# Moving the third head group's PV beside the fourth's in a fused attention and GEGLU kernel

## The chip, the cores and the metric

The kernel runs on one core of a Trainium2 chip. The metric is device time in microseconds (us) for one execution; lower is better. A core has a matrix engine (TensorE, PE in the profile, with its weight loads as PEld), a vector engine (VectorE, DVE), a scalar engine (ScalarE, ACT), a general engine (GpSimd, POOL) and a queue engine that issues DMAs (SyncE, SP). The engines run side by side, each through its own list of instructions in order, and wait for each other on semaphores. Matmuls write to PSUM, which has eight banks; a bank holds 128 x 512 float32. Only ACT and DVE copy results out of it here.

## The reference: a layernorm, a windowed attention and a GEGLU network, summed

```python
xn = layernorm(x)                                   # x: 1 x 2048 x 448, bf16
q, k, v = split_heads(xn @ wqkv)                    # 16 heads of 28
scores = einsum("bhqd,bhkd->bhqk", q, k) * 28**-0.5
mask = (i - j >= 0) & (i - j < 256)                 # sliding window of 256 keys
o = einsum("bhqk,bhkd->bhqd", softmax(where(mask, scores, -1e9)), v) @ wo
f = (gelu(xn @ w_gate) * (xn @ w_up)) @ w_down      # 448 -> 1792 -> 448
out = x + o + f
```

Each query sees at most 256 keys. The kernel takes the exponential without subtracting a maximum, and sums of the exponentials come from a column of ones that stands beside v.

## The kernel before

**Blocks.** The 2048 rows are worked in four blocks of 512 (`qb`, the loop at L740). Each block has an attention part (`attention`, L531) and a gate part (`gated`, L422). The down projection of a block (`gen_down`, L345) adds the attention output and the feed-forward output of that block in one PSUM bank, and is done in the attention part of the next block, as filling; that of the last block stands at the end of the kernel.

**Attention of a block.** The 16 heads are four groups of four. Scores, exponentials and masks are made in steps (`steps_of`, L473): nine in block 0, ten in the others. A step is a set of score matmuls into one buffer `sc` of four PSUM banks (L600), one exponential on ACT over 128 x 2048 (L604, tile `p_sb`, a ring of five buffers), then masks: in block 0 on POOL (L528), in the others three multiplications on DVE (L518), which are issued at the start of the following step. There is one `sc` buffer in this part (`score_pool(1)`), so the scores of a step wait for the exponential of the step before. In between TensorE works through `plan`, a list written out by hand with one entry per step: so many matmuls or pairs of matmuls of a generator. `(d, 5)` is five matmuls of the down projection of the block before (L359, tile `po`), `(u, 7)` or `(w, 7)` seven pairs of projections for the next block (L319, L333) or of early up pairs (`gen_up`, L401, tile `ue`). An entry `"sums"`, `"inverse"` or `"scale"` issues a part of the softmax division: `sums` (L539) transposes `oc` and takes the reciprocal on DVE, `inverse` (L547) transposes back on DVE, `scale_o` (L536) multiplies on POOL (L537) into `oN`.

**PV.** `pv(g)` (L562) multiplies the exponentials of a group with v (L570, tile `ov`). In block 0 it takes one PSUM bank and DVE copies it to `oc` (L580). In the other blocks it takes two, one for each half of the array, and `add_halves` (L553) copies the first on ACT (L554) and adds the second on DVE (L555). For group 2 and 3 of those blocks (`g > 1`) this pair is put in the list `behind` and issued at the next `flush`. `oc` has one buffer for even groups (tag `wa`) and one for odd groups (tag `wb`). The dictionary `pvs` (L585) says ahead of the scores of which step a group's PV stands: groups 0, 1 and 2 at steps 4, 6 and 9 (in block 0 at 4, 6 and 8). Group 3's PV is issued in `rest` (L629), which `gated` calls between the first gate matmuls and the first gelu (L439).

**PSUM banks.** Four banks belong to `sc`; after the last step the same four become two buffers `gt` of two banks each for the gate matmuls (`score_pool(2)`). The other four (`spare`) are handed out in turn by `take` and returned by `give` (L203, L214): to projections, down tiles, PVs and up pairs. Both lists are worked through when the program is built; on the chip a taker waits for the engine that last read the bank.

**Gate part.** A pair `p` is two of the 14 chunks of 128 hidden features. `gate(p)` is seven pairs of matmuls into `gt` (one chunk in each half of the array) and a gelu on ACT (L441); `up(p)` is seven pairs into two banks `u`; `end(p)` multiplies the two on DVE (L446 or L449) and calls `hook`, which issues parts of the softmax division by way of `after` (L639) and DMA transposes. Pairs in `early` have their up part done in attention already: 0 to 4 in block 0, 1 to 6 in block 3, none in blocks 1 and 2. The order of the gate part is written out at L454 to L471.

**Tile shapes.** A matmul can use a part of the array. The down projection and the last q projection use all of it (128 rows x 128 columns), projections, gate and up pairs half of it each (64 x 128), scores 32 x 64 (32 x 128 in block 0) and PVs 64 x 32 (128 x 32 in block 0).

Of the kernel before, what the change touches and what calls it, by code (L numbers as in the profile page):

```python
# [26 lines left out]
def kernel(  # L27
# [11 lines left out]
    nc = tc.nc  # L39
# [382 lines left out]
    def gated(qb, early, last_v, flush, hook):  # L422

        hT = hTs[qb]
        us, ges = {}, {}

        def up(p):
            if p in early:
                return
            us[p] = [take("u") for _ in range(2)]  # L430
            for c in range(7):
                chunk(us[p], wu, p, qb, c)

        def gate(p):
            gt = phase[0].pool.tile([P, 2, QB], f32, name="gt", tag="s")
            for c in range(7):
                chunk([gt[:, i, :] for i in range(2)], wg, p, qb, c)
            if not p:
                last_v()  # L439
            ges[p] = work.tile([P, 4, QB], bf16, name="p_sb", bufs=5)[:, 0:2, :]  # L440
            nc.scalar.activation(out=ges[p][:, :, :], in_=gt[:, :, :], func=ACT.Gelu_apprx_tanh)  # L441

        def end(p):
            ge = ges.pop(p)
            if p in early:
                nc.vector.tensor_tensor(out=both(hT, p), in0=ge[:, :, :], in1=both(hT, p), op=ALU.mult)  # L446
            else:
                for i, u in enumerate(us.pop(p)):
                    nc.vector.tensor_tensor(out=hT[:, p + 7 * i, :], in0=ge[:, i, :], in1=u, op=ALU.mult)  # L449
                    give(u)  # L450
                    flush()
            hook(2 * p)

        up(0)  # L454
        gate(0)
        end(0)
        gate(1)
        if 1 in early:
            end(1)
            gate(2)  # L460
            up(2)
        else:
            gate(2)
            up(1)
            end(1)
            up(2)
        end(2)
        for p in range(3, 7):
            gate(p)
            up(p)  # L470
            end(p)  # L471
# [59 lines left out]
    def attention(qb, plan):  # L531
        oN = blk.tile([P, 4, QB], bf16, name="oN")
        oNs[qb] = oN
        parts, copied, inverses, later, fresh, behind = {}, [], [], [], [], []

        def scale_o(g, oc, inv):  # L536
            nc.gpsimd.tensor_tensor(out=oN[:, g, :], in0=oc[:, :], in1=inv, op=ALU.mult)  # L537

        def sums():  # L539

            g, oc = copied.pop(0)
            l1 = work.tile([P, 16, 32], f32, name="l1", tag="wc", bufs=2)
            nc.vector.transpose(out=l1[:, :, :].rearrange("p a b -> p (a b)"), in_=oc[:, :])
            nc.vector.reciprocal(out=inv_all[:, 4 * qb + g, :], in_=l1[:, :, Dh])
            inverses.append((g, oc, l1))

        def inverse():  # L547

            g, oc, l1 = inverses.pop(0)
            nc.vector.transpose(out=l1[:, :, :], in_=inv_all[:, 4 * qb + g, :].unsqueeze(2).to_broadcast([P, 16, 32]))  # L550
            later.append((g, oc, l1[:, :, :].rearrange("p a b -> p (a b)")))

        def add_halves(oc, ov):  # L553
            nc.scalar.copy(out=oc[:, :], in_=ov[0][:, :])  # L554
            nc.vector.tensor_tensor(out=oc[:, :], in0=oc[:, :], in1=ov[1][:, :], op=ALU.add)  # L555
            give(*ov)

        def flush():
            while behind:
                add_halves(*behind.pop(0))  # L560

        def pv(g):  # L562

            ov = [take("ov") for _ in range(2 if qb else 1)]
            todo = parts.pop(g)
            for n, (half, kt, q0, nq, col, p_sb) in enumerate(todo):
                k0 = 64 * half if half else 0
                r = slice(k0, k0 + (P if half is None else 64))
                for j in range(4):
                    nc.tensor.matmul(ov[half or 0][32 * j:32 * j + 32, q0:q0 + nq], lhsT=v_sb[r, kt, 4 * g + j, :],  # L570
                                     rhs=p_sb[r, j, col:col + nq], start=n == (half or 0), stop=n + len(ov) >= len(todo),
                                     tile_position=(k0, 32 * j), skip_group_check=True)
            oc = work.tile([P, QB], f32, name="oc", tag="wb" if g % 2 else "wa", bufs=1)
            if qb:
                if g > 1:
                    behind.append((oc, ov))
                else:
                    add_halves(oc, ov)
            else:
                nc.vector.tensor_copy(out=oc[:, :], in_=ov[0][:, :])  # L580
                give(*ov)
            copied.append((g, oc))

        steps = list(steps_of(qb))
        pvs = {4: 0, 6: 1, 9: 2} if qb else {4: 0, 6: 1, 8: 2}  # L585
        for i, (scores, ncol, edges) in enumerate(steps):
            assert (qb, scores[-1][0]) in done
            if i in pvs:
                pv(pvs[i])
            while fresh:  # L590
                apply_masks(*fresh.pop(0))
            if qb == 3 and i - 1 in pvs:
                sums()
            ss = phase[0].pool.tile([P, 4, QB], f32, name="sc", tag="s")
            p_sb = work.tile([P, 4, QB], bf16, name="p_sb", bufs=5)
            for g, half, kt, q0, nq, col in scores:
                k0, nk = (64 * half, 64) if half is not None else (0, P)
                for j in range(4):
                    r = slice(32 * j, 32 * j + Dh)
                    nc.tensor.matmul(ss[k0:k0 + nk, j, col:col + nq], lhsT=kT[r, g, kt * P + k0:kt * P + k0 + nk],  # L600
                                     rhs=qT[r, g, ring(qb).start + q0:ring(qb).start + q0 + nq], start=True, stop=True,
                                     tile_position=(32 * j, k0), skip_group_check=True)
                parts.setdefault(g, []).append((half, kt, q0, nq, col, p_sb))
            nc.scalar.activation(out=p_sb[:, :, 0:ncol], in_=ss[:, :, 0:ncol], func=ACT.Exp, scale=SCALE)  # L604
            flush()
            if qb:
                fresh.append((p_sb, edges))
            else:
                for m in edges:
                    masked(p_sb, *m)  # L610
            while later:
                scale_o(*later.pop(0))
            for n in plan[i]:
                if n == "sums":
                    sums()
                elif n == "inverse":
                    inverse()
                elif n == "scale":
                    scale_o(*later.pop(0))
                if not isinstance(n, tuple):  # L620
                    if callable(n):
                        n()
                    continue
                for _ in range(n[1]):
                    next(n[0], None)
            if qb == 3 and i - 2 in pvs:
                inverse()

        def rest():  # L629
            while fresh:  # L630
                apply_masks(*fresh.pop(0))
            if not qb:
                scale_o(*later.pop(0))
                sums()
                inverse()
                scale_o(*later.pop(0))
            pv(3)

        def after(f):  # L639
            if inverses:  # L640
                inverse()
                scale_o(*later.pop(0))
            elif copied:
                sums()

        return rest, after, flush


# [25 lines left out]
    pvs = [take("pv", D)]  # L674
# [65 lines left out]
    for qb in range(NB):  # L740
# [4 lines left out]
        if qb == 0:  # L745
# [4 lines left out]
            plan = [[(u, 2), ahead, (u, 1)], [lambda: v_dense(2, pvs[2]), (u, 2), ahead2, (u, 1)],  # L750
                    [lambda: spare.append(spare.pop(1)), (u, 2), ahead3, (u, 4)], [lambda: stat(8), (u, 11)],
                    [lambda: stat(9), (u, 7), lambda: stat(10), (u, 7), lambda: fill_pads(True)], ["sums", (u, 7)],
                    ["inverse", "scale", (w, 11)], [(w, 7)],
                    [(w, 10), lambda: stat(11), lambda: rstd(8, 4), "sums", "inverse", (w, 7)]]
        else:
            d = gen_down(qb - 1)
            if qb < 3:
                u = gen_pairs(qb + 1, (("v", 0), ("k", 0), ("v", 2), ("k", 1), ("k", 2)))
                plan = [[(d, 14)], [(d, 11)], [(d, 11)], [(u, 7)], [(d, 18)], ["sums", (u, 7), "inverse"], [(u, 12)],
                        [(u, 9)], [lambda: q_last(qb + 1, nc.vector.tensor_copy), (d, 5), "sums", "inverse"], [(d, 13)]]  # L760
                if qb == 1:
                    for i in range(4):
                        plan[i].insert(0, lambda t=12 + i: stat(t))
# [4 lines left out]
            else:  # L768
                new_hT(3)
                early = (1, 2, 3, 4, 5, 6)  # L770
                u = gen_up(3, early)
                plan = [[(d, 14)], [(d, 4), (u, 5)], [(u, 9)], [(u, 7)], [(d, 18)], [(u, 7)], [(d, 13)], [(d, 5), (u, 7)],
                        [(u, 7)], [(d, 18)]]
        if qb in (1, 2):
            swap(qb + 1)
        score_pool(1)
# [171 lines left out]
```

## Time and profile before

| what | value |
|---|---|
| median of 3 runs | 216.26 us (216.24 to 216.41) |
| the profiled execution | 216.39 us |
| its span, first to last instruction | 214.7 us |
| TensorE busy | 209.1 us (97%) |
| DVE busy | 160.8 us (75%) |
| ACT busy | 130.6 us (61%) |
| POOL busy | 46.8 us (22%) |

The profile is of one execution; its rows give the start from the begin of the span, the length, the engine, the line of the kernel, and the tiles as output <- input. The difference between the execution's time and its span, 1.69 us, lies before the first and behind the last instruction. The chain of work that ended last is followed back from the last instruction, at each step to what released it or to the instruction before it on its engine. Matmuls overlap, and their ends are modelled, so the distance between starts tells more than the length of one.

### The profile page before, as it was taken

The numbers are of one execution on the slowest core, as the hardware profiler recorded it, in microseconds if no ns is written. First come the engines' busy times: TensorE is split into PE (matmuls) and PEld (weight loads), VectorE is DVE, ScalarE is ACT, GpSimd is POOL, SyncE is SP. The second block draws the span as 40 slices with busy tenths as digits, with TensorE's granted clock in tenths as the row PEclk, the third lists the DMA queues.
The fourth block names the chain that finished last, engine by engine and source line by source line (L and its number), as shares of the span: only waits on it lengthen the run. The fifth ranks groups of instructions, "written<-read, shape, count | busy, mean of one in ns | idle before, by whom it ended". The sixth has DMA issues, their size and how long they took to land.

```text
span 214.7 us, 6354 instructions
## 1 busy us (share of the span) xinstructions
PE 209.1 (97%) x2722; PEld 101.6 (47%) x2722; DVE 160.8 (75%) x357; ACT 130.6 (61%) x121; POOL 46.8 (22%) x78
## 2 busy tenths in 40 slices
PE   7999999999999999999999999999999999999993
PEld 2433444444454444444445436544444444444892
DVE  7899986999866995698546899576449699587621
ACT  4699587666767976513767897432678576466000
POOL 5287658331000211022000202022000021114001
PEclk9999999999999999999999999999999999999999
DMA  6999579993411101003230000200000000000011
GB/s 185 263 232 219 106 176 249 224 308 63 98 50 23 43 3 32 17 11 62 51 95 24 24 3 0 62 5 3 0 26 0 24 3 24 21 3 2 24 34 39
DMA packets 23297, 15.21 MB, mean 71 GB/s; under 512 B 8960, under 2 KB 23136, under 8 KB 23264
## 3 DMA queue, kind: packets, MB, share of 16 engines
q1 hardware_dynamic: 22320, 14.47, 30.0%
q8 instruction: 22, 0.36, 0.7%
q10 hardware_dynamic: 944, 0.29, 0.5%
q14 instruction: 11, 0.09, 0.2%
HBM read 9.03 MB, written 2.18 MB: 52 GB/s over the span
## 4 chain that ended last, share of the span: by engine, by line
PE 94%; DVE 1%; ACT 1%; DMA 1%; issue 1%; DVEq 0%; ACTq 0%
PE po L359 26%; PE gt L401 20%; PE u L401 12%; PE ue L401 8%; PE sc L600 6%; PE pq L333 5%; PE ov L570 5%; PE pv L319 4%; PE pq L190 2%; PE pk L333 1%; PE pv L190 1%; DMA x_sb<-in_A_x_dram 1%; ACT p_sb L604 1%; DVE st L154 1%; PE s L190 1%
## 5 line engine op out<-in xcount | busy, mean ns | idle before, releaser
L604 ACT ACTIVATE p_sb<-sc 128x2048 bf16<-128x2048 f32 x39 | 73.3, 1880 | 22.5 <-PE sc L600 15.7
L537 POOL TENSOR_TENSOR oN<-oc,l 128x512 bf16<-128x512 f32 x16 | 22.6, 1410 | 137.5 <-DVE l L550 137.5
L441 ACT ACTIVATE p_sb<-gt 128x1024 bf16<-128x1024 f32 x28 | 28.7, 1025 | 36.5 <-PE gt L401 29.6
L359 PE MATMUL po<-wd,hT 128*128 128x448 bf16 (+1 forms) x266 | 47.9, 324 | 0.0
L401 PE MATMUL gt<-xnT,wg 64*128 64x512 bf16 x224 | 45.3, 376 | 0.0
L401 PE MATMUL gt<-xsw,wg 64*128 64x512 bf16 x168 | 40.4, 376 | 0.0
L449 DVE TENSOR_TENSOR hT<-p_sb,u 128x512 bf16<-128x512 bf16 x34 | 22.0, 682 | 18.0 <-PE u L401 10.3
L518 DVE TENSOR_TENSOR p_sb<-p_sb,masks 128x256 bf16<-128x256 bf16 (+1 forms) x90 | 30.2, 391 | 4.5 <-ACT p_sb L604 4.5
L359 PEld LDWEIGHTS <-hT 128*128 128x128 bf16 x266 | 24.6, 98 | 16.2 <-issue 1.2
L401 PEld LDWEIGHTS <-wg 64*128 64x128 bf16 x392 | 19.5, 94 | 22.0 <-issue 0.2
L401 PEld LDWEIGHTS <-wu 64*128 64x128 bf16 x392 | 18.6, 94 | 23.1 <-issue 3.3
L401 PE MATMUL u<-xnT,wu 64*128 64x512 bf16 x136 | 28.2, 376 | 0.0
L401 PE MATMUL u<-xsw,wu 64*128 64x512 bf16 x102 | 24.6, 376 | 0.0
L367 DVE TENSOR_TENSOR res<-po,x_sb 128x448 bf16<-128x448 f32 (+1 forms) x17 | 10.1, 593 | 18.0 <-PE po L359 17.9
L401 PE MATMUL ue<-xnT,wu 64*128 64x512 bf16 x88 | 18.3, 377 | 0.0
L600 PE MATMUL sc<-qT,kT 28*64 28x320 bf16 (+7 forms) x648 | 16.4, 261 | 0.1
L401 PE MATMUL ue<-xsw,wu 64*128 64x512 bf16 x66 | 16.4, 377 | 0.0
L528 POOL TENSOR_SCALAR_AFFINE_SELECT p_sb<-p_sb 128x512 bf16<-128x512 bf16 (+1 forms) x21 | 14.2, 700 | 6.5 <-ACT p_sb L604 6.4
L359 PE MATMUL po<-wo,oN 128*128 128x448 bf16 (+1 forms) x76 | 15.1, 323 | 0.0
L600 PEld LDWEIGHTS <-kT 28*64 28x64 bf16 (+1 forms) x648 | 7.5, 102 | 12.6 <-issue 10.9
L418 DVE CAST hT<-ue 128x512 bf16<-128x512 f32 x20 | 12.7, 677 | 0.5 <-PE ue L401 0.4
L570 PE MATMUL ov<-p_sb,v_sb 64*32 64x320 bf16 (+7 forms) x648 | 11.7, 256 | 0.0
(102 smaller groups left out, 267.4 us busy)
## 6 DMA issues: line engine op xcount, KB each, us to landing
out_dram<-res SPq DMA_DIRECT2D x15, 112.0 KB
x_sb<-in_A_x_dram SPq DMA_DIRECT2D x3, 448.0 KB
wd<-in_B_w_down_dram SPq DMA_DIRECT2D x3, 448.0 KB
xsw<-xnT SPq DMA_DIRECT2D x6, 192.0 KB
wu<-in_B_w_up_dram SPq DMA_DIRECT2D x2, 560.0 KB
wg<-in_B_w_gate_dram SPq DMA_DIRECT2D x2, 448.0 KB
wg<-in_B_w_gate_dram SPq DMA_DIRECT2D x2, 336.0 KB
wraw<-in_A_wqkv_dram SPq DMA_DIRECT2D x2, 252.0 KB
```

What stands on the lines that cost most here:

```text
L333: nc.tensor.matmul(ps, lhsT=w.rearrange("p h d -> p (h d)"), rhs=xchunk(qb, hi, c, qb * QB, QB), start=c == 0, stop=c == 6, tile_position= ...
L359: nc.tensor.matmul(po[:, a:b], lhsT=x[:, k, cs], rhs=wt[:, k, lo + a:lo + b], start=(n == a == 0), stop=(n == len(terms) - 1), skip_group_ ...
L401: nc.tensor.matmul(ps, lhsT=w[64 * hi:64 * hi + 64, c, p * P:(p + 1) * P], rhs=xchunk(qb, hi, c, qb * QB, QB), start=c == 0, stop=c == 6, ...
L418: copy(out=hTs[qb][:, p + 7 * i, :], in_=us[i])
L441: nc.scalar.activation(out=ges[p][:, :, :], in_=gt[:, :, :], func=ACT.Gelu_apprx_tanh)
L449: nc.vector.tensor_tensor(out=hT[:, p + 7 * i, :], in0=ge[:, i, :], in1=u, op=ALU.mult)
L518: nc.vector.tensor_tensor(out=reg, in0=reg, in1=m, op=ALU.mult)
L528: nc.gpsimd.affine_select(out=reg, in_=reg, pattern=mid + [[1 if diag else -1, min(w, P)]], compare_op=ALU.is_ge, fill=0.0, base=0 if diag ...
L537: nc.gpsimd.tensor_tensor(out=oN[:, g, :], in0=oc[:, :], in1=inv, op=ALU.mult)
L570: nc.tensor.matmul(ov[half or 0][32 * j:32 * j + 32, q0:q0 + nq], lhsT=v_sb[r, kt, 4 * g + j, :], rhs=p_sb[r, j, col:col + nq], start=n == ...
L600: nc.tensor.matmul(ss[k0:k0 + nk, j, col:col + nq], lhsT=kT[r, g, kt * P + k0:kt * P + k0 + nk], rhs=qT[r, g, ring(qb).start + q0:ring(qb) ...
L604: nc.scalar.activation(out=p_sb[:, :, 0:ncol], in_=ss[:, :, 0:ncol], func=ACT.Exp, scale=SCALE)
```

## The change

Four edits that belong together.

- `pvs` loses group 2, and `rest` issues `pv(2)` directly ahead of `pv(3)`: both now stand behind the matmuls of gate pair 0. Only group 3 (`g > 2`) is put in `behind`; the copy and the add of group 2 follow its PV at once.
- In `gated` gate pairs 0 and 1 stand first, then up pair 0, then the rest as before.
- `rest` no longer makes the sums, the inverse and the scaling of group 2 in block 0; the ends of the gate pairs do, as in the other blocks.
- Block 0: three pairs of matmuls move from step 8 to step 7. Blocks 1 and 2: one down matmul moves from step 9 to step 8. Block 3: three up pairs move from step 7 to step 8.

```diff
@@ gated
+        gate(0)
+        gate(1)
         up(0)
-        gate(0)
         end(0)
-        gate(1)
         if 1 in early:
             end(1)
             gate(2)
-            up(2)
         else:
             gate(2)
             up(1)
             end(1)
-            up(2)
+        up(2)
         end(2)
@@ pv
             if qb:
-                if g > 1:
+                if g > 2:
                     behind.append((oc, ov))
@@ attention
-        pvs = {4: 0, 6: 1, 9: 2} if qb else {4: 0, 6: 1, 8: 2}
+        pvs = {4: 0, 6: 1}
@@ rest
             while fresh:
                 apply_masks(*fresh.pop(0))
-            if not qb:
+            while later:
                 scale_o(*later.pop(0))
-                sums()
-                inverse()
-                scale_o(*later.pop(0))
+            pv(2)
             pv(3)
@@ plan, block 0 (steps 7 and 8)
-                    ["inverse", "scale", (w, 11)], [(w, 7)],
-                    [(w, 10), lambda: stat(11), lambda: rstd(8, 4), "sums", "inverse", (w, 7)]]
+                    ["inverse", "scale", (w, 11)], [(w, 10)],
+                    [lambda: stat(11), (w, 7), lambda: rstd(8, 4), "sums", "inverse", (w, 7)]]
@@ plan, blocks 1 and 2 (steps 8 and 9)
-                        [(u, 9)], [lambda: q_last(qb + 1, nc.vector.tensor_copy), (d, 5), "sums", "inverse"], [(d, 13)]]
+                        [(u, 9)], [lambda: q_last(qb + 1, nc.vector.tensor_copy), (d, 6), "sums", "inverse"], [(d, 12)]]
@@ plan, block 3 (steps 7 and 8)
-                plan = [[(d, 14)], [(d, 4), (u, 5)], [(u, 9)], [(u, 7)], [(d, 18)], [(u, 7)], [(d, 13)], [(d, 5), (u, 7)],
-                        [(u, 7)], [(d, 18)]]
+                plan = [[(d, 14)], [(d, 4), (u, 5)], [(u, 9)], [(u, 7)], [(d, 18)], [(u, 7)], [(d, 13)], [(d, 5), (u, 4)],
+                        [(u, 10)], [(d, 18)]]
```

## The prediction, made before the changed kernel was built

> **What bounds the kernel now.** The first view is the page: part 1 (busy time), the clock row of part 2 and the shares of the chain in part 4.
>
> ```profile
> span 214.7 us, 6354 instructions
> ...
> PE 209.1 (97%) x2722; PEld 101.6 (47%) x2722; DVE 160.8 (75%) x357; ACT 130.6 (61%) x121; POOL 46.8 (22%) x78
> ...
> PEclk9999999999999999999999999999999999999999
> ...
> PE 94%; DVE 1%; ACT 1%; DMA 1%; issue 1%; DVEq 0%; ACTq 0%
> ```
>
> TensorE is busy for 209.1 of 214.7 us, its clock is full in every slice, and the chain of work that ended last runs on it for 94% of the span. So there are nearly no holes to close: a change can win only if TensorE spends less time on the same matmuls. The diff adds and removes no matmul, so I looked in the chain for time that TensorE spends without streaming columns. The second view is that chain, in order of time, at the end of attention of block 1, where the diff cuts (start, length, line):
>
> ```profile
> 76.14 0.38 PE sc L600 x16
> ...
> 77.48 0.95 PE po L359 x5
> 78.43 0.68 PE ov L570 x40
> 79.11 0.34 PE sc L600 x16
> 79.46 2.58 PE po L359 x13
> 82.04 1.63 PE u L401 x14
> 83.66 1.51 PE gt L401 x14
> 85.17 0.66 PE ov L570 x40
> 85.83 3.14 PE gt L401 x28
> ```
>
> The reader is to see three things. There is no gap: from 77.48 on each piece begins where the last ends. Seven pairs of gate or up matmuls take 1.51 us when they follow others of the same tile shape (the gt at 83.66), so a pair of 512 columns streams in 1.51/7 = 0.216 us. But the same seven pairs take 1.63 at 82.04, where they follow the down projection, which uses the whole array: **a change of tile shape costs 1.63 - 1.51 = 0.12 us**. The PV pieces say the same: by the code a PV of blocks 1 to 3 streams 512 + 512 + 256 = 1280 columns in each half of the array, which at 0.216 per 512 is 0.54 us, and the piece lasts 0.68 (behind po) or 0.66 (behind gt). So 0.14 us of a PV is its change of shape, in whichever row it is booked.
>
> **The change, part by part.** *The third group's PV goes behind the fourth's gate.* Before, step 9 runs po, ov, sc, po and later gt, ov, gt: six changes of shape, counting po to u. After, it is po, sc, po, gt, ov, ov, gt: five. What goes is one change per block: 0.68 - 0.54 = 0.14 us in each of blocks 1 to 3. No row of before shows two PVs side by side, so I bound that seam. At best it costs nothing, as u to gt does, and a change might cost as much as the dearest first up pair, 1.68 (below) - 1.51 = 0.17. At worst the seam costs a full change and the block gains nothing. I take a seam of zero, that is 0.14, because gt behind u is the nearest row: another tile, another PSUM bank, the same shape. The Trainium skill, TensorEngine Tiling (Array Packing), under Key Properties, says that changing the tiling mode, "not just tile", drains TensorE; that would make the seam free. No row here shows that seam itself.
>
> *Block 0.* Here there is a second loss. The timeline shows it on TensorE and then on DVE (start, length, engine, line, count, in brackets the idle time before and who ended it); behind them stand further rows of the chain, which this and the next parts use.
>
> ```profile
> 35.01 0.38 PE L333 MATMUL pq<-xnT,wqp 64*128 64x512 bf16 x1
> 35.34 0.37 PE L333 MATMUL pk<-xsw,wsq 64*128 64x512 bf16 x1
> ...
> 38.16 0.38 PE L401 MATMUL gt<-xnT,wg 64*128 64x512 bf16 x1
> 38.36 0.40 PE L401 MATMUL gt<-xsw,wg 64*128 64x512 bf16 x2
> ```
>
> ```profile
> 32.66 1.16 DVE L226 CAST v_sb<-pv 128x448 bf16<-128x448 f32 x2 [0.60 <-PE pv L319]
> 34.59 0.69 DVE L580 COPY oc<-ov 128x512 f32<-128x512 f32 x1 [0.78 <-POOL oN L537]
> ```
>
> ```profile
> 31.62 0.33 PE sc L600 x8
> ...
> 33.49 0.60 PE ov L570 x16
> 34.09 0.33 PE sc L600 x8
> ...
> 40.03 0.60 PE ov L570 x20
> ...
> 132.48 1.68 PE u L401 x14
> ...
> 174.67 0.35 PE sc L600 x16
> ...
> 177.69 0.35 PE sc L600 x16
> 178.04 1.62 PE ue L401 x14
> 179.66 0.68 PE ov L570 x40
> 180.34 0.34 PE sc L600 x16
> 180.69 3.53 PE po L359 x18
> ```
>
> The two halves of a pair normally start together. At 35.01 pq starts, but its partner pk only at 35.34, and at 38.16 and 38.36 they are still apart; only the PV, a change of shape, brings them together. Following `take` and `give` by hand, pk of group 1 gets the bank in which the third group's PV has just been. That bank is free when L580 has copied it, 34.59 + 0.69 = 35.28, and L580 was held for 0.78 by POOL's scaling of L537, which releases the `wa` buffer. In the chain, from the end of the scores (34.09 + 0.33 = 34.42) to the PV stand 3 + 7 + 7 pairs of projections and 7 of gates: 24 x 0.216 = 5.18, so 39.60, and with 0.12 for the change of shape 39.72. The PV started at 40.03: **0.31 us lost**. After the change no PV stands there. Group 1 takes two banks of the second v pair, copied out by 32.66 + 1.16 = 33.82, and the skew has no cause. The PV of block 0 streams 384 + 384 + 256 + 128 = 1152 columns, 0.48 us, of a piece of 0.60, so its change of shape is 0.12. Block 0 gains 0.12 + 0.31 = 0.43.
>
> *Fills moved.* A PV stood between two score steps as cover for the exponential that must end before the next scores can use the single score buffer. Where it goes, the interval shrinks, and the fills of the diff put part of it back. How short may it be? ACT's rows in block 3, where the intervals are shortest (start, length):
>
> ```profile
> 160.58 1.88 ACT L604 ACTIVATE p_sb<-sc 128x2048 bf16<-128x2048 f32 x1 [0.54 <-PE sc L600]
> 163.00 1.88 ACT L604 ACTIVATE p_sb<-sc 128x2048 bf16<-128x2048 f32 x1 [0.54 <-PE sc L600]
> ```
>
> 163.00 - 160.58 = 2.42: 1.88 of exponential and 0.54 until the next starts. I take that for the floor; it may be a little lower, which would only help. Blocks 1 and 2, step 8: scores stand at 76.14 and 79.11, 2.97 apart; without the PV (0.68) and with one more po (2.58/13 = 0.20) it is 2.49, above the floor by 0.07. Blocks 0 and 3, from the chain's rows above: block 0, step 7: 34.09 - 31.62 = 2.47, less 0.60 and with three pairs (0.65) 2.52: above. Block 3, step 7: 177.69 - 174.67 = 3.02, less three pairs 2.37: **below by 0.05**, a stall of that size. Step 8: 180.34 - 177.69 = 2.65, less 0.68 and with 0.65, 2.62: above. So the fills cost 0.05 in all, at most 0.2 if my intervals are 0.1 too long in blocks 1 and 2.
>
> *First gate instead of the first up pair behind the last step.* Gate 0 uses the score buffer's banks, so it waits for the last exponential, where up pair 0 did not. In block 1 the last scores move from 79.11 to 79.11 - 0.48 = 78.63; gate 0 follows after 0.34 of scores and 12 po at 2.58/13, that is 2.72, at 81.35. The exponential begins at most 0.54 behind the start of the scores (the floor leaves 0.54 for release and scores together) and ends by 78.63 + 0.54 + 1.88 = 81.05. Cover of 0.30: no cost; without it, each us of delay costs a us in blocks 1 and 2. What the edit moves on ACT is one copy of the PV (L554), which now stands ahead of the first gelu instead of ahead of the table load; gate 2 is the first to need that gelu, some 4 us later (two PVs, gate 1, up 0). Up pair 0 takes the banks of the third group's PV, and between that PV and it lie the other PV (0.54) and gate 1 (1.51), 2.05 in all, against a copy on ACT and an add on DVE, by L580's 0.69 some 1.4 (an estimate from that row). No DMA is moved past another; the stores and the k3 round trip keep their order.
>
> *Sums, inverse and scaling in block 0* move from ahead of the fourth PV to the ends of gate pairs, as in the other blocks. They leave DVE's queue where PV copies wait; TensorE needs the scaled result only in block 1's first down projection. Cost nothing.
>
> *Sum:* 0.43 + 0.14 + 0.14 + (0.14 - 0.05) = 0.80 us. The profiled execution took 216.39 us (the span and 1.69 around it), so 215.59 in its terms. The median of the runs is 216.26, 0.13 lower; I take the 0.80 from that: **215.5 us**, 0.37% faster. By the ends for the seam: all at zero gain in blocks 1 to 3 and in block 0, 0.31 - 0.05 = 0.26, so 216.0; all at 0.17, 0.94, so 215.3. Less than 0.2%, 0.43 us, can hardly be told from no change here, so faster means under 215.83.
>
> **The rivals.** *A: a PV is bound by its instructions, not by columns and a drain.* Then two side by side last twice one, and only the bank wait of block 0 goes: 216.26 - 0.26 = 216.0, no change by the bound. For it: the weight loads of one PV alone, in block 2, last 0.56.
>
> ```profile
> 128.80 0.56 PEld L570 LDWEIGHTS <-v_sb 64*32 64x32 bf16 x48 [0.37 <-issue]
> ```
>
> Against it: block 0's PV with less than half of the matmuls (16 in the row at 33.49, 40 at 179.66) takes 0.60 to 0.68, and scores of 8 matmuls 0.33 to the 0.35 of 16: the length follows columns, not instructions. The Trainium skill, TensorE: Matmul & The Clock Gate, under "Wait — 56ns, not 53.3ns?", states that matmuls never start less than about 25 ns apart; 48 would then need about 1.2 us, an estimate from that page. The trace disagrees: the whole piece lasts 0.68.
>
> *B: the last masks become late, and the kernel slower.* The fourth PV needs the masks of step 9, which stand on DVE behind those of step 8 and the last down tile's add:
>
> ```profile
> 79.81 1.86 DVE L518 TENSOR_TENSOR p_sb<-p_sb,masks 128x256 bf16<-128x256 bf16 x3
> ...
> 82.58 0.62 DVE L367 TENSOR_TENSOR res<-po,x_sb 128x448 bf16<-128x448 f32 x1
> 83.11 0.82 DVE L518 TENSOR_TENSOR p_sb<-p_sb,masks 128x256 bf16<-128x256 bf16 x3
> ...
> 181.53 1.86 DVE L518 TENSOR_TENSOR p_sb<-p_sb,masks 128x256 bf16<-128x256 bf16 x3
> ```
>
> ```profile
> 79.96 1.56 POOL L537 TENSOR_TENSOR oN<-oc,l 128x512 bf16<-128x512 f32 x1 [6.92 <-DVE l L550]
> ```
>
> Three masks take 0.82, or 1.86 beside POOL's scaling. After the change, in block 1: masks of step 8 until 79.81 + 1.86 = 81.67, the add until 82.29, the last masks until 83.11. TensorE reaches the fourth PV at 81.35 + 1.51 + 0.68 = 83.54. Margin 0.43. If the last masks, too, took 1.86, the PV would be 0.61 late in blocks 1 and 2. In block 3 the same count gives 181.53 + 1.86 + 0.62 + 1.86 = 185.87 for the masks and (180.34 - 0.68 + 0.34 + 3.53 + 1.51 + 0.68) 185.72 for the PV, 0.15 late. In all 1.37, so 216.8. It decides from a total lateness of 1.23 (0.80 + 0.43). Against it: the scaling starts 0.15 behind the masks of step 8 and lasts 1.56, so it is over before the last masks begin.
>
> *C: block 0's wait comes back at another bank.* Then 0.31 is not gained: 0.49, 215.8, on the edge of the bound. Against it: the new PVs take banks whose copies were issued more than a microsecond earlier.
>
> **How the numbers follow.** Forecast 0.66, A 0.16, C 0.06, B 0.12. The forecast's own range is 215.2 to 215.8. With A, C and some slack for a partly late mask the range is 215.2 to 216.4; B's 216.8 stays outside. Faster: 0.66 and half of C, 0.69; same: A and half of C, 0.19; slower: B, 0.12.
>
> **What would show it.** In the chain of the changed kernel: one PV piece per block of 1.2 us (forecast) or 1.35 (A); no po–ov–sc in step 9; in block 0 both halves of every pair start together from 34 to 39 us, and the PV ends some 0.4 us earlier. Exponentials 2.42 apart would mark fills that are too short. Idle TensorE time ahead of the fourth PV, ended by DVE L518, would be B; ahead of gate 0, ended by ACT, a fault in my cover of 0.30. I am wrong altogether if the pieces without a change of shape grow.

## The result, and the profile after

The changed kernel takes 215.61 us (median of 13 runs, 215.44 to 215.97) against 216.26 (216.06 to 216.59): a ratio of 0.9969, with a 95% interval of 0.9961 to 0.9978. A second measurement gave 0.9971 (0.9962 to 0.9980). The change makes the kernel 0.65 us faster; 0.80 was forecast.

The page of the changed kernel, the same rows as before:

```profile
span 214.0 us, 6358 instructions
...
PE 208.4 (97%) x2722; PEld 100.8 (47%) x2722; DVE 161.9 (76%) x357; ACT 130.3 (61%) x121; POOL 46.7 (22%) x78
```

The 2722 matmuls are the same, and TensorE is busy for 0.7 us less: 208.4 against 209.1. The span is shorter by the same 0.7. So the time came out of TensorE's busy time, as argued, and not out of gaps. (Busy time holds time in which only one half of the array worked; block 0 is such a case.) (Lines of the file behind L453 shift: scores are now L599, PV L569, masks L517, the PV's add L554.)

Where did it come from? The chain of each kernel, cut at the first scores of blocks 1, 2 and 3 and at the last down projection; before:

```profile
52.83 0.35 PE sc L600 x16
...
104.08 0.35 PE sc L600 x16
...
154.57 0.35 PE sc L600 x16
...
197.18 13.88 PE po L359 x126
```

and after:

```profile
52.38 0.35 PE sc L599 x16
...
103.57 0.35 PE sc L599 x16
...
153.91 0.35 PE sc L599 x16
...
196.52 13.87 PE po L359 x126
```

Subtracting gives a lead of 0.45 at the end of block 0, 0.51 after block 1, 0.66 after block 2 and 0.66 at the last down projection. By block that is **0.45, 0.06, 0.15 and 0.00**. The forecast was 0.43, 0.14, 0.14 and 0.09.

Block 1 of the changed kernel, in the chain, from step 8 to the first up pair:

```profile
78.18 0.38 PE sc L599 x17
78.56 2.39 PE po L359 x12
80.95 1.62 PE gt L401 x14
82.57 1.26 PE ov L569 x81
83.82 1.62 PE gt L401 x14
85.44 1.51 PE u L401 x14
```

The reader is to see one PV piece of 1.26 us where there were two of 0.68 and 0.66. The change of shape behind po now falls on the first gate (1.62) instead of the first up pair (1.63). The up pair behind gate 1 takes 1.51, so its banks were free in time. The scores of step 9 take 0.38 instead of 0.34.

Block 0:

```profile
31.61 0.33 PE sc L599 x8
...
34.13 0.33 PE sc L599 x8
...
37.59 1.51 PE gt L401 x14
39.10 1.09 PE ov L569 x36
```

The two PVs take 1.09 against 0.60 + 0.60. (The count of a row of the chain can leave out matmuls; the trace has 36 in this pair and 96 in that of block 1.) From the end of the scores (34.46) to gate 0 are 3.13, for 14 pairs of projections: 0.216 each and 0.11 for the change of shape. The timeline shows the two halves of each pair starting together, here the first pair of group 1, which had parted before, and the first pair of gate 0:

```profile
34.39 0.39 PE L333 MATMUL pq<-xnT,wqp 64*128 64x512 bf16 x1
34.39 0.39 PE L333 MATMUL pk<-xsw,wsq 64*128 64x512 bf16 x1
...
37.42 0.38 PE L401 MATMUL gt<-xnT,wg 64*128 64x512 bf16 x1
37.42 0.59 PE L401 MATMUL gt<-xsw,wg 64*128 64x512 bf16 x2
```

Block 3, where nothing was gained:

```profile
174.00 0.35 PE sc L599 x16
...
176.38 0.03 issue
176.41 0.42 PE sc L599 x16
...
179.09 0.34 PE sc L599 x16
```

TensorE stops for 0.03 ahead of the scores at 176.41, and these take 0.42 instead of 0.35, because they wait for the exponential: 0.10 between them. Not all of this is new: in blocks 2 and 3 the scores at 126.02 and 159.43 stand 2.41 behind those before them and take 0.42, and in the kernel before their like at 126.53 and 160.09 do so too. These waits the change leaves as they were.

The masks of the last step, on which rival B hung, in DVE's timeline of block 1:

```profile
79.37 1.86 DVE L517 TENSOR_TENSOR p_sb<-p_sb,masks 128x256 bf16<-128x256 bf16 x3
...
81.69 0.81 DVE L517 TENSOR_TENSOR p_sb<-p_sb,masks 128x256 bf16<-128x256 bf16 x3
```

They end at 82.50, when the third PV has just begun and over half a microsecond ahead of the fourth.

### The profile page after: what moved, and what is told of

The parts are those of the page before. It is cut to its first block, busy times and chain, and to the rows that moved or that the text cites. A ratio compares the mean times of both kernels' runs of the same rounds, so it can differ in the third digit from the quotient of the medians.

```text
span 214.0 us, 6358 instructions
## 1 busy us (share of the span) xinstructions
PE 208.4 (97%) x2722; PEld 100.8 (47%) x2722; DVE 161.9 (76%) x357; ACT 130.3 (61%) x121; POOL 46.7 (22%) x78
## 4 chain that ended last, share of the span: by engine, by line
PE 94%; DVE 1%; ACT 1%; DMA 1%; issue 1%; DVEq 0%; ACTq 0%
PE po L359 26%; PE gt L401 20%; PE u L401 12%; PE ue L401 8%; PE sc L599 7%; PE pq L333 7%; PE ov L569 5%; PE pv L319 4%; PE pq L190 2%; PE pv L190 1%; DMA x_sb<-in_A_x_dram 1%; ACT p_sb L603 1%; DVE st L154 1%; PE s L190 1%; PE pk L190 1%
## 5 line engine op out<-in xcount | busy, mean ns | idle before, releaser
L517 DVE TENSOR_TENSOR p_sb<-p_sb,masks 128x256 bf16<-128x256 bf16 (+1 forms) x90 | 30.1, 389 | 4.5 <-ACT p_sb L603 4.5
L401 PEld LDWEIGHTS <-wg 64*128 64x128 bf16 x392 | 18.6, 94 | 23.0 <-issue 1.3
L599 PE MATMUL sc<-qT,kT 28*64 28x320 bf16 (+7 forms) x648 | 16.4, 261 | 0.1
L599 PEld LDWEIGHTS <-kT 28*64 28x64 bf16 (+1 forms) x648 | 7.7, 102 | 13.5 <-issue 12.2
L554 DVE TENSOR_TENSOR oc<-oc,ov 128x512 f32<-128x512 f32 x12 | 8.2, 686 | 4.8 <-ACT oc L553 4.7
```

The costliest lines, as they stand in the source:

```text
L401: nc.tensor.matmul(ps, lhsT=w[64 * hi:64 * hi + 64, c, p * P:(p + 1) * P], rhs=xchunk(qb, hi, c, qb * QB, QB), start=c == 0, stop=c == 6, ...
L517: nc.vector.tensor_tensor(out=reg, in0=reg, in1=m, op=ALU.mult)
```

## The experiments

The theory tested: block 0's gain is mostly the bank wait, blocks 1 to 3 gain a change of shape less something at the seam, and the fills decide whether the rest arrives. The chief rival: the gain is the change of shape alone, alike in each block, and the fills are of little account. "Before" in the ratios is the kernel before, run on the same chip beside the kernels of a group.

**Each half of the change alone.** The first kernel applies all edits in block 0 and leaves the others as before; the second does the opposite. In the diffs only the conditions are shown.

```diff
@@ e1_block0_alone, against before
+        pvs = {4: 0, 6: 1, 9: 2} if qb else {4: 0, 6: 1}
...
+            if not qb:
+                while later:
+                    scale_o(*later.pop(0))
+                pv(2)
             pv(3)
...
+        if not qb:
+            gate(0)
+            gate(1)
+            up(0)
...
@@ e2_blocks123_alone, against the changed kernel
+        pvs = {4: 0, 6: 1} if qb else {4: 0, 6: 1, 8: 2}
```

> The change in block 0 alone; blocks 1 to 3 as before. My theory: block 0 gains 0.45 us, 0.31 of it the wait for a bank and 0.12 a change of tile shape, so 216.26 - 0.45 = 215.8, and block 1's first scores stand at 52.38 instead of 52.83 in the chain. Rival: the gain is spread evenly over the blocks because it comes from the change of shape alone; then 216.26 - 0.65/4 = 216.1.

> The change in blocks 1 to 3 alone; block 0 as before. My theory: two PVs side by side take 1.26 instead of 0.68 + 0.66, 0.08 less per block, and of these 0.24 block 3 gives back 0.10 at its short fill, so 0.1 to 0.2 in all, 216.1. Forecast as it stood: 0.14 per block less 0.05, that is 215.9. Rival: nothing comes from these blocks, 216.26.

Measured: block 0 alone 215.72 against 216.20, ratio 0.9979 (0.9968 to 0.9991); blocks 1 to 3 alone 216.02, ratio 0.9991 (0.9982 to 1.0000). The two gains, 0.48 and 0.18, add up to 0.66, the whole of it. Block 0 carries some 70%, so the even spread of the rival is out. The second interval touches no change, so its size rests on the chain, where the last down projection of that kernel stands at 197.06 with block 1 beginning at 52.92:

```profile
52.92 0.35 PE sc L615 x16
...
197.06 13.88 PE po L359 x126
```

That is 144.14 us for blocks 1 to 3, against 197.18 - 52.83 = 144.35 before and 144.14 in the changed kernel. The 0.21 is the same with or without the edit in block 0.

**Is it the bank?** This kernel is the one before with one edit: the copy of group 2's PV in block 0 has a buffer of its own, so that it does not wait for POOL to release the shared one. The PV stays in its old place.

```diff
-            oc = work.tile([P, QB], f32, name="oc", tag="wb" if g % 2 else "wa", bufs=1)
+            oc = work.tile([P, QB], f32, name="oc", tag="wb" if g % 2 else "wa" if qb or not g else "wz", bufs=1)
```

> The kernel before with a buffer of its own for oc of group 2 in block 0, so that its copy out of the bank no longer waits for POOL; the PV stays where it was. My theory: the two halves of the pairs start together again and block 0 gains 0.31: 215.95. Rival: the skew is not what costs, the block gains only where the PV moves: 216.26.

Measured: 216.06 against 216.20, ratio 0.9993 (0.9984 to 1.0002), half of what I expected and not clear of no change. The profile shows why. The copy now starts as soon as the PV ends, both halves go on together, and the gates behind the fourth PV start in the chain at 40.32 instead of 40.03 + 0.60 = 40.63, the 0.31 that the theory wants. DVE's timeline has the copy:

```profile
34.13 0.69 DVE L580 COPY oc<-ov 128x512 f32<-128x512 f32 x1 [0.33 <-PE ov L570]
```

But the five gate pairs behind it take 7.84 instead of 7.66, because one waited for its weights (the chain, then the view of waits: who waited, on what, us in total, times, longest):

```profile
40.32 7.84 PE gt L401 x70
```

```profile
PEld L401 <- DMA wg<-in_B_w_gate_dram: 0.3, 1, 0.3
```

TensorE had become early enough to meet a DMA. (The changed kernel, which is earlier still at these gates, at 40.19, shows no such wait in its profile; why its weights were there in time is open.) The next kernel adds one edit to this one, which puts the load of these weights two places forward in SP's queue, and the x rows of block 3 behind the up weights.

```diff
         load_ffn(wg, B_w_gate, slice(0, 3))
-        nc.sync.dma_start(out=x_sb[:, 12:16, :], in_=xv[:, 12:16, :])
-        load_ffn(wu, B_w_up, slice(5, 7))
         load_ffn(wg, B_w_gate, slice(3, 7))
+        load_ffn(wu, B_w_up, slice(5, 7))
+        nc.sync.dma_start(out=x_sb[:, 12:16, :], in_=xv[:, 12:16, :])
```

> The kernel before with the own buffer for oc of group 2 in block 0, and the gate weights of pairs 3 to 6 loaded ahead of the x rows of block 3 and the last up weights. In e3_own_buffer gate 1 began 0.32 earlier, but a gate pair then waited for its weights and only 0.14 was left at block 1's first scores. My theory: with the weights there in time all of the 0.31 arrives, 216.2 - 0.3 = 215.9. Rival: the late pair waits for something else and the time stays that of e3_own_buffer, 216.06.

Measured: 215.99 against 216.34, ratio 0.9983 (0.9974 to 0.9992). The gates are back at 7.66:

```profile
31.70 0.33 PE sc L600 x8
...
40.41 7.66 PE gt L401 x70
...
52.61 0.35 PE sc L600 x16
```

From the scores of step 7 to block 1 this is 20.91, against 52.83 - 31.62 = 21.21 before and 52.38 - 31.61 = 20.77 in the changed kernel. So of block 0's 0.44, **0.30 is the wait for one PSUM bank**, which a 2 KB buffer per partition also removes, and 0.14 is left for the change of shape; the PV rows alone show 0.11 of it (1.20 - 1.09). The order of the weights was not run alone on the kernel before. On the changed kernel it brought nothing in block 0: the same stretch takes 20.78 with it (31.73 to 52.51, in the last version below) and 20.77 without it (31.55 to 52.32, in the changed kernel run beside that version).

**The fills.** The changed kernel with the fills of before:

```diff
-                    ["inverse", "scale", (w, 11)], [(w, 10)],
-                    [lambda: stat(11), (w, 7), lambda: rstd(8, 4), "sums", "inverse", (w, 7)]]
+                    ["inverse", "scale", (w, 11)], [(w, 7)],
+                    [lambda: stat(11), (w, 10), lambda: rstd(8, 4), "sums", "inverse", (w, 7)]]
...
-                        ... (d, 6), "sums", "inverse"], [(d, 12)]]
+                        ... (d, 5), "sums", "inverse"], [(d, 13)]]
...
-                ... [(d, 5), (u, 4)],
-                        [(u, 10)], [(d, 18)]]
+                ... [(d, 5), (u, 7)],
+                        [(u, 7)], [(d, 18)]]
```

> The changed kernel with the fills of before: three pairs back to step 8 in block 0, one down matmul back to step 9 in blocks 1 and 2, three up pairs back to step 7 in block 3. My theory, with a floor of 2.42 from one exponential to the next: block 0 2.47 - 0.60 = 1.87, 0.5 lost; blocks 1 and 2 2.97 - 0.68 = 2.29, 0.15 lost each; block 3 at step 8 2.65 - 0.68 = 1.97, 0.45 lost, and 0.10 regained at step 7; 1.1 in all, 215.6 + 1.1 = 216.7, slower than before. Rival: the fills matter little since TensorE does the same work and waits are made up later: 215.7.

Measured: 216.97 against 216.20, ratio 1.0036 (1.0022 to 1.0050), slower than before. Against the changed kernel that is 1.4 us, more than the 1.1 worked out. The chain shows the exponential itself on the path, at step 9 of block 3:

```profile
178.16 0.40 PE sc L599 x16
...
178.63 1.89 ACT p_sb L603
...
180.56 0.41 PE sc L599 x17
```

From scores to scores 2.40: the floor of 2.42 was right. What was not in my working is that scores which wait take longer: those at 180.56 take 0.41 instead of 0.34. (The 0.40 at 178.16 is another matter: there the chain goes on through the exponential, so its row runs to the end of the last matmul and not to the next one's start.) The move of a few matmuls is worth twice what the change itself brings.

**One up pair of block 3 back.** From 4 and 10 to 5 and 9.

> The changed kernel with one up pair of block 3 back from step 8 to step 7 (5 and 9 instead of 4 and 10). My theory: scores of step 8 no longer wait for the exponential, which cost 0.10, and step 9 stays above the floor (2.62 - 0.21 = 2.41, at the edge): 215.5. Rival: step 9 now waits instead, 215.6.

Measured: 215.79 against 216.34, ratio 0.9982 (0.9969 to 0.9994), not distinct from the changed kernel. The rival was right: step 8 no longer waits, and step 9 does. The chain has the scores of step 8 at 0.35 and those of step 9 at 0.41:

```profile
176.61 0.35 PE sc L599 x16
...
179.02 0.41 PE sc L599 x17
179.43 3.53 PE po L359 x18
```

The po behind it starts at 179.43, as in the changed kernel (179.09 + 0.34). Two steps share too little filling, and moving it between them moves the wait.

**The order of gates and up pair.** The changed kernel with up pair 0, gate 0, both PVs, then gate 1, as the gate part stood before.

> The changed kernel with the order of before at the start of the gate part: up pair 0, gate 0, both PVs, the ends, gate 1. My theory: up pair 0 holds two of the four banks, so the fourth PV waits until ACT has copied and DVE has added the third's, some 0.6 + 0.7 us and the releases between, 1.4 to 1.6 in each of blocks 1 to 3: 215.6 + 4.5 = 220.1. Rival: the order of up and gate is of no account, 215.6.

Measured: 220.48 against 216.34, ratio 1.0191 (1.0176 to 1.0206), 4.8 us more than the changed kernel, 1.6 in each of three blocks. The chain of block 1:

```profile
84.07 0.75 PE ov L570 x40
...
84.84 0.59 ACT oc L554
...
85.46 0.70 DVE oc L555
...
86.20 0.73 PE ov L570 x32
```

The fourth PV stands behind the copy on ACT and the add on DVE, because up pair 0 holds the other two banks. Two PVs of blocks 1 to 3 can only be neighbours where all four banks are free: the second edit of the change is a condition of the first.

**What the seam costs.** Two PVs took 1.26, not 0.68 + 0.54 = 1.22, nor the 1.20 of 0.14 below 1.34. In this kernel the matmuls of group 3's PV are issued twice in blocks 1 to 3, the second time over the first, so that three stand in a row.

```diff
             todo = parts.pop(g)
+            if qb and g == 3:
+                todo = todo + todo
...
-                                     rhs=p_sb[r, j, col:col + nq], start=n == (half or 0), stop=n + len(ov) >= len(todo),
+                                     rhs=p_sb[r, j, col:col + nq], start=n % 12 == (half or 0), stop=n + len(ov) >= len(todo),
```

> The changed kernel with the matmuls of group 3's PV issued twice in blocks 1 to 3, the second time over the first, so three PVs stand side by side. My theory: the 0.06 that the pair of PVs takes beyond its columns is paid once, when the matmuls of the second begin to start 8 to 9 ns apart instead of 3 to 4; a third then adds its columns alone, 0.56: pieces of 1.82 instead of 1.26, 215.6 + 1.7 = 217.3. Rival: each seam between two PVs costs 0.06: 1.88, 217.5. If the third added 0.68, a seam would be a full change of shape.

Measured: pieces of 1.81 in all three blocks.

```profile
80.98 1.62 PE gt L401 x14
82.60 1.81 PE ov L571 x121
84.41 1.62 PE gt L401 x14
```

A third PV adds 0.55: its columns alone (0.54). So this second seam is free, and what the second PV takes too much is paid once per row of PVs. The rival's 0.06 per seam would have given 1.88. The time, 218.15 (ratio 1.0096, 1.0072 to 1.0119), is 2.5 above the changed kernel instead of 1.7: besides the three PVs, in the profile gate 1 of block 3 takes 2.58 instead of 1.62, with a stop of 0.58 in it that is put down to "issue" and for which the profile names no releaser. Its cause was not followed up.

**A version with the waits mended.** The changed kernel with the weights order above, one down matmul moved from step 6 to step 7 of block 3 (12 and 6), and one more from step 9 to step 8 in blocks 1 and 2 (11 and 7); beside it, on the same chip, the changed kernel again.

> The changed kernel with three small moves that the runs suggest: block 3 takes one down matmul from step 6 to step 7 (12 and 6), blocks 1 and 2 one more from step 9 to step 8 (11 and 7), and the gate weights of pairs 3 to 6 are loaded ahead of the x rows of block 3. My theory: the waits of the scores for the exponential go, 0.10 in block 3 and 0.04 in block 1, so 0.14 less than the changed kernel on the same chip, some 215.5. Rival: as in e7_block3_fill the wait moves on to the next step and the time stays.

> The changed kernel as it is, on the same chip as e8_best, as the measure for it: 0.9969 of the kernel before, some 215.6.

Measured: 215.58 (0.9966, 0.9954 to 0.9978) and 215.58 (0.9971, 0.9962 to 0.9980). The profile has the waits gone in both places; block 3:

```profile
173.89 0.35 PE sc L599 x16
...
176.45 0.35 PE sc L599 x16
```

A filling taken from a step with slack to spare removes the wait, where one moved between two tight steps did not. From the first scores of block 1 to the last down projection the chain is 0.15 us shorter (196.50 - 52.51 = 143.99, against 196.46 - 52.32 = 144.14 in the changed kernel run beside it). But that is 0.07%, less than this measurement can tell, and the medians are equal. Nothing beyond the changed kernel is claimed.

## Why the prediction was right

**What bounds it.** Right. The matmuls are the same, and TensorE's busy time fell by what the span fell.

**Block 0.** Right in size and cause: 0.43 forecast, 0.44 to 0.45 measured. The bank wait, read off a pair that started 0.33 apart and a copy that waited for POOL, is 0.31 at the gates by the run that removed only that wait, and 0.30 at block 1 once the weights were early too. How the 0.31 is lost can be read off two more rows of the kernel before, the pair behind the parted one:

```profile
35.34 0.39 PE L333 MATMUL pq<-xsw,wsq 64*128 64x512 bf16 x1
35.55 0.37 PE L333 MATMUL pk<-xnT,wkp 64*128 64x512 bf16 x1
```

The half that was on time starts its next matmul 0.33 behind the last instead of 0.22, so 0.11 is lost at once. From there on the other half runs about 0.20 behind it (35.34 and 35.55, 38.16 and 38.36), and this 0.20 is lost at the PV. What I had not seen is the DMA right behind the wait: rival C guessed another bank, while in that run the next thing in the way is the weights of a later gate pair.

**The change of shape in blocks 1 to 3.** The mechanism was right and its size was off: 0.14 forecast, 1.34 - 1.26 = 0.08 measured; the 1.26 lies between the forecast's 1.2 and rival A's 1.35, nearer the first. That another PV as such costs nothing, as the third PV in a row shows, agrees with the rule of the Trainium skill (TensorEngine Tiling (Array Packing), Key Properties) that another tile alone drains nothing. But a row of two PVs pays 0.06 once. In the trace, starts of single matmuls lie 3 to 4 ns apart within a set of eight through all of the first PV; from about the fiftieth matmul on they lie 8 to 9 ns apart, up to the last set of the second PV, in each of blocks 1 to 3 and in no PV that stands alone (48 matmuls). Block 0's pair has 36 matmuls in all, shows no such slowing, and gains its full 0.11 (1.20 - 1.09). That the slower starts make the end late is the reading that fits these rows; it was not tested by itself. Nor is it shown what sets them off: the fiftieth matmul is also the second one of the second PV, so a count of instructions and the place cannot be told apart, and block 0's tiles are of another shape. The weight loads slow to 8 or 9 ns before the matmuls do, from the 44th on, and the last five of the third group's PV do so in the kernel before, too, where it stands alone. Rival A was wrong as it stood, since a PV's length follows its columns, but it may hold a grain: the rate of instructions may matter in a longer row. The 25 ns between matmuls of the Trainium skill (TensorE: Matmul & The Clock Gate, "Wait — 56ns, not 53.3ns?") doesn't hold for such tiles: 3 to 4 and 8 to 9 ns here.

**The fills.** Forecast 0.05, measured 0.10 in block 3 and 0.04 in block 1 (0.38 against 0.34). The floor was right, 2.40 to 2.42; the term that the prediction put at nothing is the 0.04 to 0.07 by which scores that have waited run longer. Block 1's interval came out as worked out (78.18 - 75.70 = 2.48, forecast 2.49), and its scores ran longer all the same. That the fills are what makes the change pay is shown: with the old ones it is 0.77 us slower than the kernel before.

**A gain not in the sum.** Block 2 gained 0.15 where 0.08 can be accounted for. Its first up pair behind the down projection took 1.68, and the two halves began 0.08 apart:

```profile
132.41 0.39 PE L401 MATMUL u<-xnT,wu 64*128 64x512 bf16 x1
132.49 0.53 PE L401 MATMUL u<-xsw,wu 64*128 64x512 bf16 x2
```

It was the same kind of skew as in block 0; the first gate, which stands there now, takes 1.62. I had this row as an upper bound for a change of shape. Its cause was a bank, too, as the trace has it: the late matmul waits for ACT, whose copy out of the third PV's first bank was due then (131.85 + 0.58 = 132.43).

```profile
131.85 0.58 ACT L554 COPY oc<-ov 128x512 f32<-128x512 f32 x1
```

No run separated its price from the rest. That these 0.06 were not in the sum is luck that makes up for part of the two terms that were too good.

**The sum.** 0.45 + (0.08 - 0.04 + 0.02) + (0.08 + 0.06) + (0.08 - 0.10 + 0.02) = 0.65, with 0.02 for gate and up pieces that differ by 0.01 each; the chain gives 0.66 and the medians 0.65.

**Rival B and the covers.** The last masks were over 0.5 us early in each of blocks 1 to 3, and gate 0 (1.62, a plain change of shape) did not wait for the exponential. Up pair 0 found its banks free. These steps held, and the run with the old gate order shows what the bank order is worth: 1.6 us per block.

## What to carry to other kernels

Where one engine is busy all the time, ask of each piece how long its columns alone would take; the rest was here change of tile shape and two halves out of step, and both could be moved or removed without touching the work. A block of work that is moved away from between two steps was also cover for something: count the interval that is left against the measured floor, and fill it from a step with slack, not from its neighbour. And look at what the faster path meets next: here, in one profile, TensorE met a DMA after 0.13 of the 0.31 us that it had gained.

## What the runs showed of the hardware that was not expected

- One half of the array began 0.33 us late (35.01 and 35.34 in the kernel before). It held the other back by 0.11 at the next pair, and the 0.20 between them stayed through the 20 pairs that follow; only the next change of tile shape joined them, and there the lag was paid.
- In a row of small tile matmuls (64 x 32, eight at a time) starts lie 3 to 4 ns apart up to about the fiftieth, where the second PV begins, and 8 to 9 ns behind it; such a row takes 0.06 us more than its parts, once. That the one causes the other was not tested.
- Scores that had waited for an exponential took 0.38 to 0.42 us in blocks 1 to 3, the scores without a wait 0.34 to 0.37.
